# Decode attention with a gated unit on one core: keys multiplied in whole blocks, values by four columns of weights, the gate's weights late

## The chip, the cores and the metric

The kernel runs on one core of a Trainium2 chip. The metric is the device time of one execution in microseconds. Three runs of the kernel before took 719.57, 720.96 and 721.34 us; the median is 720.96.

## The reference

One token passes a block of attention over a cache and a gated unit; the product of the two is added to the input. All is in 32-bit floats.

```python
xn = layernorm(x)                                        # x: 1 x 512
q  = (xn @ wq).reshape(32, 128)                          # 32 heads of 128
p  = softmax(einsum("hd,hkd->hk", q, k_cache) * 128**-0.5)   # 8192 keys a head
s  = einsum("hk,hkd->hd", p, v_cache).reshape(4096) @ wo # 4096 x 512
h  = sigmoid(xn @ w_gate) * (xn @ w_up)                  # 512 x 1376 each
g  = silu(h @ w_down)                                    # 1376 x 512
out = x + s * g
```

K and V caches have 4096 KB for each head, 268.4 MB in all; the weights add 25.2 MB (wq and wo 8.39 MB each, the three of the gated unit 8.46 MB together).

## The kernel before

All large inputs pass through one pool of six slots (`stream`, 128 partitions x 32 KB): a slot holds one head's K, one head's V, half of `wq`, half of `wo`, or one of the three weights of the gated unit. SyncE issues every load, in the order in which the program names them, and stops at a load for which no slot is free; the loads behind it then stop too. The order is x, both halves of `wq`, `w_gate`, `w_up`, `w_down`, then K and V head by head, with K of the last two heads ahead of their V, and `wo` in two halves last. The second half of `wo` is cut into three loads. `need` issues along this order up to the item that is asked for; at head h the program asks for K of head h + 2.

A tile of K has 64 rows of keys in each partition (128 x 64 = 8192 keys), 128 elements each. The engines' instructions are issued in the order of the program (`manual_schedule`); semaphores between them come from the accesses to tiles.

For the start, VectorE and TensorE normalise x, TensorE multiplies it with `wq` (L152) and spreads four heads' queries at a time over all partitions (`spread`, L159 to L165). The gated unit follows as a whole: 11 blocks of columns of each of the two weights are loaded into TensorE as 128 x 128 blocks and multiplied by one column (L179), then sigmoid and product, and the product with `w_down` (L189 to L193).

Then the heads run, a head's second part behind the first quarter of the next head's scores:

- `scores` (L205 to L212): for each of the 64 rows of keys VectorE multiplies by the query and sums up in one fused operation (L211), which puts the products into a scratch tile and one score per partition into `sc`; the profile shows it as two instructions, the operation and a read of its sum.
- `row_max` and `all_max` (L214 to L228): the maximum of a partition's scores, TensorE's transpose of these 128 values, their maximum, its spread over the partitions, and ScalarE's exponential with the sum of each partition.
- `values` (L230 to L246): the total of the sums by a product with ones (`pl`), its reciprocal, and 64 products, each with one column of `pr` as weights (loaded into TensorE) and 128 columns of V moving; four groups of TensorE's columns take them in turn. ScalarE copies the four partial rows, and four small products with the reciprocal turn them into a column (`o_all`).

In the last step `project` multiplies the 32 heads with `wo` (L251, 128 products), and VectorE multiplies by the gate and adds x (L300, L301). The heads' order and the six slots set what TensorE, VectorE and the loads may do at one time: a slot of K comes free behind the last score of its head, a slot of V behind the last of its 64 products.

## Time and profile before

| | before |
|---|---|
| median of three runs | 720.96 us |
| profiled execution, its own time | 719.32 us |
| span of the profile, first to last instruction | 717.5 us |
| TensorE matmuls, busy | 334.6 us, 47% |
| VectorE, busy | 460.1 us, 64% |
| ScalarE, busy | 43.6 us, 6% |
| bytes read from the memory | 293.67 MB, 409 GB/s over the span |
| mean granted TensorE clock | 0.650 of full speed |

Times of the rows below count from the start of the span. A group's row gives line, engine, operation, the tiles out<-in, shapes and count, then busy time, mean duration of one in ns, and the idle time of the engine before it with what ended it. PE is TensorE's matmul, PEld its weight load, DVE VectorE, ACT ScalarE, SPq SyncE's queue. A matmul of 32-bit floats shows as two instructions.

### The profile page before, as it was taken

Reading aid. Unit: us, or ns where it says so; the run is one execution under the profiler, and the core shown is the slowest. Engines: PE = TensorE matmul, PEld = TensorE weight load, DVE = VectorE, ACT = ScalarE, POOL = GpSimd, SP = SyncE. Lnnn points to the kernel's source line nnn. Section 1 sums busy time; section 2 is a strip of 40 time slices with the busy share of each in tenths; the row PEclk is TensorE's granted clock in tenths of the full one; section 3 lists DMA queues with packets and bytes.
Section 4 is the critical chain, followed back from the end, with each engine's and each line's share of the span. In section 5 each row is a group of like instructions: output and inputs, shape, how many; then the busy total and the mean of one; then the engine's idle time right before and its main releaser. Section 6 shows DMA issues by size and latency. Waiting matters only on the chain.

```text
span 717.5 us, 15014 instructions
## 1 busy us (share of the span) xinstructions
PE 334.6 (47%) x5148; PEld 233.7 (33%) x5148; DVE 460.1 (64%) x4213; ACT 43.6 (6%) x177; POOL 0.7 (0%) x6
## 2 busy tenths in 40 slices
PE   3799155455444453235444453335444442234466
PEld 1499033333233332122333332223333221222345
DVE  1000888887767766667677666677677666676860
ACT  0100010000000000000000000000000000000000
POOL 0000000000000000000000000000000000000000
PEclk9855556655666666666665555555555666666659
DMA  9999999999999999999999999999999999999930
GB/s 378 419 433 434 428 425 432 436 435 425 431 429 435 432 429 427 436 429 438 426 427 434 432 434 427 431 432 434 429 431 427 436 432 432 407 424 420 400 158 21
DMA packets 11500, 294.63 MB, mean 411 GB/s; under 512 B 1336, under 2 KB 1344, under 8 KB 1696
## 3 DMA queue, kind: packets, MB, share of 16 engines
q1 hardware_dynamic: 11424, 293.68, 95.6%
q8 instruction: 40, 0.66, 0.3%
q14 instruction: 36, 0.29, 0.1%
HBM read 293.67 MB, written 0.00 MB: 409 GB/s over the span
## 4 chain that ended last, share of the span: by engine, by line
DMA 64%; DVE 24%; PE 9%; ACT 1%; issue 1%; SPq 0%; DVEq 0%
DMA k<-in_A_k_cache_dram 55%; DVE junk L211 22%; PE pgu L179 5%; DMA wo<-in_A_wo_dram 5%; DMA wg<-in_B_w_gate_dram 4%; PE pl L232 1%; PE pm L224 1%; DVE sc L211 1%; ACT pr L228 1%; PE po L237 1%; PE pd L189 1%; PE acc L251 1%; DVE mx L222 0%; ACT mx L225 0%; DVE rl L234 0%
## 5 line engine op out<-in xcount | busy, mean ns | idle before, releaser
L211 DVE CUSTOM_DVE_ANT_0 junk<-k,qb 128x128 f32<-128x128 f32 x2048 | 439.7, 288 | 99.8 <-DMA k<-in_A_k_cache_dram 99.8
L237 PE MATMUL po<-v,pr 128*1 128x128 f32 x4096 | 184.1, 362 | 0.0
L211 DVE DVE_READ_ACCUMULATOR2_ANT sc<- 128x1 f32 x2048 | 170.2, 83 | 0.1
L237 PEld LDWEIGHTS po<-v,pr 128*1 128x1 f32 x4096 | 126.4, 110 | 48.8 <-issue 0.2
L224 PE MATMUL pm<-mx,ones 1*128 1x1 f32 x64 | 18.6, 357 | 182.9 <-DVE mx L222 182.9
L224 PEld LDWEIGHTS pm<-mx,ones 1*128 1x128 f32 x64 | 15.9, 306 | 205.5 <-DVE mx L222 205.5
L218 PE MATMUL pt<-ident,mx 128*1 128x128 f32 x64 | 17.6, 375 | 138.7 <-DVE mx L216 138.7
L218 PEld LDWEIGHTS pt<-ident,mx 128*1 128x1 f32 x64 | 2.8, 80 | 141.8 <-DVE mx L216 126.2
L234 DVE RECIPROCAL rl<-pl 128x1 f32<-128x1 f32 x32 | 5.4, 169 | 65.0 <-PE pl L232 65.0
L183 DVE TENSOR_TENSOR hid<-hid,pgu 128x10 f32<-128x10 f32 (+1 forms) x2 | 0.3, 159 | 62.6 <-ACT hid L182 62.6
L232 PE MATMUL pl<-rs,ones 128*128 128x1 f32 x64 | 18.7, 362 | 24.7 <-ACT pr L228 24.7
L245 PE MATMUL pT<-rl,o 128*32 128x1 f32 x256 | 20.5, 201 | 12.6 <-ACT o L240 12.6
L245 PEld LDWEIGHTS pT<-rl,o 128*32 128x32 f32 x256 | 17.8, 154 | 22.0 <-ACT o L240 22.0
L232 PEld LDWEIGHTS pl<-rs,ones 128*128 128x128 f32 x64 | 16.0, 310 | 27.5 <-ACT pr L228 27.5
L225 ACT ACTIVATE mx<-pm 128x1 f32<-128x1 f32 x32 | 5.5, 171 | 318.8 <-PE pm L224 318.8
L240 ACT COPY o<-po 128x128 f32<-128x128 f32 x32 | 8.5, 266 | 204.7 <-PE po L237 204.7
L179 PEld LDWEIGHTS pgu<-xn,wg 128*128 128x128 f32 (+1 forms) x88 | 19.4, 316 | 1.1 <-ACT q_row L155 1.1
L179 PE MATMUL pgu<-xn,wg 128*128 128x1 f32 (+1 forms) x88 | 19.5, 358 | 0.3 <-DMA wg<-in_B_w_gate_dram 0.3
L179 PE MATMUL pgu<-xn,wu 128*128 128x1 f32 (+1 forms) x88 | 19.5, 358 | 0.0
L179 PEld LDWEIGHTS pgu<-xn,wu 128*128 128x128 f32 (+1 forms) x88 | 19.4, 317 | 0.0
L152 PE MATMUL pq<-wq,xn 128*1 128x512 f32 x64 | 10.3, 800 | 13.6 <-DMA wq<-in_A_wq_dram 13.6
L162 PE MATMUL pb<-q_row,ones 1*128 1x512 f32 x16 | 15.6, 1074 | 0.0
(46 smaller groups left out, 83.4 us busy)
## 6 DMA issues: line engine op xcount, KB each, us to landing
k<-in_A_k_cache_dram SPq DMA_DIRECT2D x32, 4096.0 KB, 44.7
v<-in_A_v_cache_dram SPq DMA_DIRECT2D x32, 4096.0 KB, 38.7
wq<-in_A_wq_dram SPq DMA_DIRECT2D x2, 4096.0 KB, 16.6
wo<-in_A_wo_dram SPq DMA_DIRECT2D x1, 4096.0 KB, 44.8
wo<-in_A_wo_dram SPq DMA_DIRECT2D x1, 3072.0 KB, 36.8
wg<-in_B_w_gate_dram SPq DMA_DIRECT2D x1, 2752.0 KB
wu<-in_B_w_up_dram SPq DMA_DIRECT2D x1, 2752.0 KB, 34.1
wd<-in_B_w_down_dram SPq DMA_DIRECT2D x1, 2560.0 KB, 40.0
```

What stands on the lines that cost most here:

```text
L152: nc.tensor.matmul(pq[b][g * GP:g * GP + 1, :], xn[:, k:k + 1], wq_t[k][:, c:c + QT], start=(k == 0), stop=(k == KT - 1))
L162: nc.tensor.matmul(pb, ones[g * GP:g * GP + 1, :], q_row[g * GP:g * GP + 1, b, :], start=True, stop=True)
L179: nc.tensor.matmul(pgu[:m, a * NT + t:a * NT + t + 1], gl[name, k][:, cols], xn[:, k:k + 1], start=(k == 0), stop=(k == KT - 1))
L189: nc.tensor.matmul(pd[g * GP:g * GP + 1, :GC], hid[:m, t:t + 1], gl["wd", t][:m, g * GC:(g + 1) * GC], start=(t == 0), stop=(t == NT - 1))
L211: nc.vector.tensor_tensor_reduce(junk, kv_t["k", h][:, j, :], q, 1.0, 0.0, ALU.mult, ALU.add, sc[h][:, j:j + 1])
L218: nc.tensor.matmul(pt, mx[h][:, 0:1], ident, start=True, stop=True)
L224: nc.tensor.matmul(pm, ones[:1, :], mx[h][:1, 1:2], start=True, stop=True)
L228: nc.scalar.activation(pr[h], sc[h], AF.Exp, bias=mx[h][:, 2:3], scale=SCALE, accum_out=rs[h])
L232: nc.tensor.matmul(pl, ones, rs[h], start=True, stop=True)
L237: nc.tensor.matmul(po[h % 2][g * GP:g * GP + 1, :], pr[h][:, j:j + 1], kv_t["v", h][:, j, :], start=(j < NG), stop=(j >= NB - NG))
L240: nc.scalar.copy(o1, po[h % 2])
L245: nc.tensor.matmul(pT[rows, r:r + 1], o1[:, r:Dh:R], rl[h], start=True, stop=True)
```

## The change

- The fused operation on 128 elements is replaced by two on 16 rows of keys at once: a product of 2048 elements written in place over the K tile, with the query repeated by a stride of zero, and a sum over each of the 16 rows. A head has four such pairs (SB = 16).
- The values take four columns of `pr` as weights and 512 columns of V moving, 16 products a head. Each gives four rows, of which only the diagonal blocks are wanted; four products with `pick`, which has a one at the wanted row of each group, add these up into one partition of `pn`, one for each of four heads. The sums go into a column of the same tile. Every fourth head `heads_out` divides, and VectorE's own transposes make the column `o_all`.
- The gated unit's weights are loaded between the heads, behind V of heads 20, 21 and 22; its products run between heads 21 and 25, with xn as weights and the columns of `w_gate` and `w_up` moving. Sigmoid and product use spare room in the slots of these two weights. K and V of the first two heads follow `wq` at once.
- The load of x as rows comes late, behind most of `wo`, and the last load of `wo` is cut at partition 120. `wo` stays last. The small tiles of PSUM have one buffer in place of three.

```diff
--- before.py
+++ after.py
@@ -35,17 +35,16 @@
...
+    SB = 16
-    R = 4
-    NW = H // R
-    FT = F // P
-    FL = F - FT * P
+    NW = H // HT
     SCALE = float(Dh) ** -0.5
+    GLU = 20
...
-    ps_s = ctx.enter_context(tc.tile_pool(name="ps_s", bufs=3, space=bass.MemoryType.PSUM))
+    ps_s = ctx.enter_context(tc.tile_pool(name="ps_s", bufs=1, space=bass.MemoryType.PSUM))

...
     def load_gate(name, src):
-        t = slot(name)[:, :KT * F].rearrange("p (k f) -> p k f", f=F)
+        t = slot(name)
+        gl[name, "spare"] = t[:, KT * F:KT * F + QT]
+        t = t[:, :KT * F].rearrange("p (k f) -> p k f", f=F)
         nc.sync.dma_start(t, src.rearrange("(p k) f -> p k f", k=KT))
         for k in range(KT):
             gl[name, k] = t[:, k, :]

+
...
     def load_down():
...
+        t = slot("wd")[:, :NF * D].rearrange("p (c e) -> p c e", e=D)
+        c = 0
+        for f0, m, r in FB:
+            nc.sync.dma_start(t[:m, c:c + r, :],
+                              w_down[f0:f0 + m * r, :].rearrange("(p r) e -> p r e", r=r))
+            c += r
+        gl["wd"] = t

     def load_rows(which, src, h):
         t = slot(f"{which}{h}")
         nc.sync.dma_start(t, src[0, h].rearrange("(p j) d -> p (j d)", p=P))
...
+        if last:
+            nc.sync.dma_start(t[:, m, :HT - 1, :], src[:, m, :HT - 1, :])
+            nc.sync.dma_start(x_row[0:P:GP, :], xv.rearrange("(g c) -> g c", g=NG))
+            for p0, p1 in ((0, 120), (120, P)):
+                nc.sync.dma_start(t[p0:p1, m, HT - 1, :], src[p0:p1, m, HT - 1, :])
...
+    order = [("wq", 0), ("wq", 1)]
+    for h in range(H):
+        order.append(("k", h))
+        if h < H - 2:
+            order.append(("v", h))
+        if GLU <= h < GLU + 3:
+            order.append(("glu", h - GLU))
+    order += [("v", H - 2), ("v", H - 1), ("wo", 0), ("wo", NW // 2)]
+
+    def issue(which, i):
+        if which == "wq":
+            load_wq(i)
+        elif which == "wo":
+            load_wo(i, NW // 2, i > 0)
+        elif which == "glu":
+            (lambda: load_gate("wg", w_gate), lambda: load_gate("wu", w_up), load_down)[i]()
+        else:
+            load_rows(which, k_cache if which == "k" else v_cache, i)
+
...
     nc.sync.dma_start(x_col, xv.rearrange("(p k) -> p k", k=KT))
-    load_wq(0)
-    nc.vector.memset(x_row, 0.0)
-    nc.sync.dma_start(x_row[0:P:GP, :], xv.rearrange("(g c) -> g c", g=NG))
-    load_wq(1)
-    load_gate("wg", w_gate)
-    load_gate("wu", w_up)
-    load_down()
+    need("v", 1)


...
+    nc.vector.memset(x_row, 0.0)

...
-    hid = const.tile([P, FT + 1], F32, name="hid")
+
     g_row = const.tile([P, GC], F32, name="g_row")
-    pgu = ps_big.tile([P, 512], F32, tag="ps_big", name="pgu")
-    NT = FT + 1
-    for a, name in enumerate(("wg", "wu")):
-        for t in range(NT):
-            m = P if t < FT else FL
-            cols = slice(t, FT * P, FT) if t < FT else slice(FT * P, F)
-            for k in range(KT):
-                nc.tensor.matmul(pgu[:m, a * NT + t:a * NT + t + 1], gl[name, k][:, cols], xn[:, k:k + 1],
+    pgu = {}
+
+    def glu_row(name):
+        pgu[name] = big(f"p{name}", 0.0)
+        for k in range(KT):
+            for n, f0 in enumerate(range(0, F, QT)):
+                w = min(QT, F - f0)
+                nc.tensor.matmul(pgu[name][n * GP:n * GP + 1, :w], xn[:, k:k + 1], gl[name, k][:, f0:f0 + w],
                                  start=(k == 0), stop=(k == KT - 1))
-    for rows, c0, c1 in ((P, 0, FT), (FL, FT, NT)):
-        nc.scalar.activation(hid[:rows, c0:c1], pgu[:rows, c0:c1], AF.Sigmoid)
-        nc.vector.tensor_mul(hid[:rows, c0:c1], hid[:rows, c0:c1], pgu[:rows, NT + c0:NT + c1])
-    pd = ps_big.tile([P, 512], F32, tag="ps_big", name="pd")
-    nc.vector.memset(pd[:, :GC], 0.0)
-    for t in range(NT):
-        m = P if t < FT else FL
-        for g in range(NG):
-            nc.tensor.matmul(pd[g * GP:g * GP + 1, :GC], hid[:m, t:t + 1],
-                             gl["wd", t][:m, g * GC:(g + 1) * GC],
-                             start=(t == 0), stop=(t == NT - 1))
-    nc.scalar.activation(g_row, pd[:, :GC], AF.Sigmoid)
-    nc.vector.tensor_mul(g_row, g_row, pd[:, :GC])
+
+    def glu_hidden():
+        nc.scalar.activation(gl["wg", "spare"], pgu["wg"], AF.Sigmoid)
+        nc.vector.tensor_mul(gl["wu", "spare"], gl["wg", "spare"], pgu["wu"])
+
+    def glu_out():
+        ph = big("ph")
+        hid = const.tile([P, NF], F32, name="hid")
+        c = 0
+        for f0, m, r in FB:
+            n, o = divmod(f0, QT)
+            row = gl["wu", "spare"][n * GP:n * GP + 1]
+            for t in range(r):
+                nc.tensor.matmul(ph[:m, c + t:c + t + 1], row[:, o + t:o + m * r:r],
+                                 ones[n * GP:n * GP + 1, 0:1], start=True, stop=True)
+            nc.scalar.copy(hid[:m, c:c + r], ph[:m, c:c + r])
+            c += r
+        pd = big("pd", 0.0)
+        c = 0
+        for f0, m, r in FB:
+            for t in range(c, c + r):
+                for g in range(NG):
+                    nc.tensor.matmul(pd[g * GP:g * GP + 1, :GC], hid[:m, t:t + 1],
+                                     gl["wd"][:m, t, g * GC:(g + 1) * GC],
+                                     start=(t == 0), stop=(t == NF - 1))
+            c += r
+        nc.scalar.activation(g_row, pd[:, :GC], AF.Sigmoid)
+        return pd


     acc = ps_acc.tile([P, GC], F32, name="acc")
     nc.vector.memset(acc, 0.0)
-    po = [ps_o.tile([P, Dh], F32, name=f"po{i}") for i in range(2)]
+    po = [ps_o.tile([P, QT], F32, name=f"po{i}") for i in range(2)]
+
+    pn = [ps_o.tile([P, Dh + 1], F32, name=f"pn{i}") for i in range(2)]
     for t in po:
         nc.vector.memset(t, 0.0)
-
-    o_all = const.tile([P, NW, R], F32, name="o_all")
-    sc, mx, pr, rs, rl = {}, {}, {}, {}, {}
+    for t in pn:
+        nc.vector.memset(t, 0.0)
+        nc.vector.memset(t[:, Dh:], 1.0)
+
+    o_all = const.tile([P, NW, HT], F32, name="o_all")
+
+    pick = const.tile([P, HT], F32, name="pick")
+    nc.vector.memset(pick, 0.0)
+    for g in range(NG):
+        nc.vector.tensor_copy(pick[g * GP:(g + 1) * GP, :], ident[g * GP:(g + 1) * GP, g * GP:g * GP + HT])
+    sc, mx, pr, rs = {}, {}, {}, {}

     def scores(h, j0, j1):
         if j0 == 0:
             sc[h] = work.tile([P, NB], F32, tag="sc", name=f"sc{h}")
-        q = qb[h // HT][:, (h % HT) * Dh:(h % HT + 1) * Dh]
-        for j in range(j0, j1):
-            junk = work.tile([P, Dh], F32, tag="junk", name=f"junk{h}_{j}")
-            nc.vector.tensor_tensor_reduce(junk, kv_t["k", h][:, j, :], q, 1.0, 0.0, ALU.mult, ALU.add,
-                                           sc[h][:, j:j + 1])
+        q = qb[h // HT][:, (h % HT) * Dh:(h % HT + 1) * Dh].rearrange("p (o d) -> p o d", o=1)
+        q = q.to_broadcast([P, SB, Dh])
+        for j in range(j0, j1, SB):
+            kt = kv_t["k", h].rearrange("p (j d) -> p j d", d=Dh)[:, j:j + SB, :]
+            nc.vector.tensor_mul(kt, kt, q)
+            nc.vector.reduce_sum(sc[h][:, j:j + SB], kt, axis=AX.X)

     def row_max(h):
         mx[h] = work.tile([P, 4], F32, tag="mx", name=f"mx{h}")
@@ -228,71 +292,70 @@
         nc.scalar.activation(pr[h], sc[h], AF.Exp, bias=mx[h][:, 2:3], scale=SCALE, accum_out=rs[h])

     def values(h):
-        pl = ps_s.tile([P, 1], F32, tag="ps_s", name=f"pl{h}")
-        nc.tensor.matmul(pl, ones, rs[h], start=True, stop=True)
-        rl[h] = work.tile([P, 1], F32, tag="rl", name=f"rl{h}")
-        nc.vector.reciprocal(rl[h], pl)
-        for j in range(NB):
-            g = j % NG
-            nc.tensor.matmul(po[h % 2][g * GP:g * GP + 1, :], pr[h][:, j:j + 1], kv_t["v", h][:, j, :],
-                             start=(j < NG), stop=(j >= NB - NG))
-        o1 = work.tile([P, Dh], F32, tag="o1", name=f"o1_{h}")
+        w, i = divmod(h, HT)
+        row = pn[w % 2][i * GP:i * GP + 1, :]
+        nc.tensor.matmul(row[:, Dh:], rs[h], ones[:, 0:1], start=True, stop=True)
+
+        for j in range(0, NB, HT):
+            g = j // HT % NG
+            nc.tensor.matmul(po[h % 2][g * GP:g * GP + HT, :], pr[h][:, j:j + HT],
+                             kv_t["v", h][:, j * Dh:(j + HT) * Dh],
+                             start=(j < HT * NG), stop=(j >= NB - HT * NG))
+        o1 = work.tile([P, QT], F32, tag="o1", name=f"o1_{h}", bufs=1)
         nc.scalar.copy(o1, po[h % 2])
-        w, i = divmod(h, R)
-        pT = ps_s.tile([P, R], F32, tag="ps_s", name=f"pT{h}")
-        rows = slice(i * GP, (i + 1) * GP)
-        for r in range(R):
-            nc.tensor.matmul(pT[rows, r:r + 1], o1[:, r:Dh:R], rl[h], start=True, stop=True)
-        nc.scalar.copy(o_all[rows, w, :], pT[rows, :])
+        for b in range(HT):
+            nc.tensor.matmul(row[:, :Dh], pick[:, b:b + 1], o1[:, b * Dh:(b + 1) * Dh],
+                             start=(b == 0), stop=(b == HT - 1))
+
+    def heads_out(w):
+        rl = work.tile([P, 1], F32, tag="rl", name=f"rl{w}")
+        nc.vector.reciprocal(rl, pn[w % 2][:, Dh:])
+        on = work.tile([P, Dh], F32, tag="on", name=f"on{w}", bufs=1)
+        nc.vector.tensor_scalar(on, pn[w % 2][:, :Dh], rl, None, op0=ALU.mult)
+        ot = work.tile([P, HT, GP], F32, tag="ot", name=f"ot{w}", bufs=1)
+        for r in range(HT):
+            nc.vector.transpose(ot[:, r, :], on[:, r:Dh:HT])
+        nc.vector.tensor_copy(o_all[:, w, :], ot[:, :, 0])

     def project(w):
-        for r in range(R):
+        for r in range(HT):
             for g in range(NG):
                 nc.tensor.matmul(acc[g * GP:g * GP + 1, :], o_all[:, w, r:r + 1],
                                  wo_t[w][:, r, g * GC:(g + 1) * GC],
-                                 start=(w + r == 0), stop=(w == NW - 1 and r == R - 1))
-
-
-    order = []
+                                 start=(w + r == 0), stop=(w == NW - 1 and r == HT - 1))
+
+
+    spread(0)
+    pt = pd = None
     for h in range(H):
-        order.append(("k", h))
-        if h < H - 2:
-            order.append(("v", h))
-    order += [("v", H - 2), ("v", H - 1), ("wo", 0), ("wo", NW // 2)]
-
-    def issue(item):
-        which, i = item
-        if which == "wo":
-            load_wo(i, NW // 2, () if i == 0 else ((0, R - 1), (R - 1, R)))
-        else:
-            load_rows(which, k_cache if which == "k" else v_cache, i)
-
-    ahead = iter(order)
-    loaded = set()
-
-    def need(item):
-        while item not in loaded:
-            nxt = next(ahead)
-            issue(nxt)
-            loaded.add(nxt)
-
-    pt = None
-    for h in range(H):
-        need(("k", h))
+        need("k", h)
         if h + 2 < H:
-            need(("k", h + 2))
+            need("k", h + 2)
         if h % HT == HT - 2 and h + HT < H:
             spread(h // HT + 1)
-        scores(h, 0, NB // 4)
+        scores(h, 0, SB)
         if h > 0:
             all_max(h - 1, pt)
-            need(("v", h - 1))
+            if h % HT == 1 and h > 1:
+                heads_out(h // HT - 1)
+            need("v", h - 1)
             values(h - 1)
-        scores(h, NB // 4, NB)
+        scores(h, SB, NB)
         pt = row_max(h)
-    need(order[-1])
+        if h == GLU + 1:
+            glu_row("wg")
+        elif h == GLU + 2:
+            glu_row("wu")
+        elif h == GLU + 3:
+            glu_hidden()
+        elif h == GLU + 4:
+            pd = glu_out()
+        elif h == GLU + 5:
+            nc.vector.tensor_mul(g_row, g_row, pd[:, :GC])
+    need(*order[-1])
     all_max(H - 1, pt)
     values(H - 1)
+    heads_out(NW - 1)
     for w in range(NW):
         project(w)

```

## Rows read from the trace of the kernel before

**Rows 1.** Busy time of each engine, clock and transfers in two stretches.

```profile
core 0: us, PE busy (x) PEld busy (x) DVE busy (x) ACT busy (x) POOL busy (x), PEclk, DMA share, GB/s
500.00:600.00 100.00, 42.97 (x712) 28.72 (x712) 71.27 (x655) 5.74 (x26) 0.00 (x0) 0.62 1.00 431
692.00:710.00 18.00, 11.71 (x270) 8.91 (x270) 3.53 (x31) 1.03 (x5) 0.00 (x0) 0.72 0.07 30
```

**Rows 2.** Timeline of SyncE's queue: start us, us, what; two issues of K.

```profile
556.87 0.33 SPq L91 DMA_DIRECT2D k<-in_A_k_cache_dram  x1
...
577.18 0.33 SPq L91 DMA_DIRECT2D k<-in_A_k_cache_dram  x1
```

**Rows 3.** Chain that ended last, from head 30 on: start us, us, what.

```profile
617.78 44.73 DMA k<-in_A_k_cache_dram
...
662.64 0.29 DVE junk L211
...
673.66 36.81 DMA wo<-in_A_wo_dram
...
710.51 3.72 PE acc L251 x128
```

**Rows 4.** Loads by tile: KB each, median us from issue to landing.

```profile
x_col<-in_A_x_dram SPq DMA_DIRECT2D x1, 2.0 KB, 1.6
```

**Rows 5.** The page: engines' busy us (share) xinstructions; transfer queues: packets, MB, share.

```profile
PE 334.6 (47%) x5148; PEld 233.7 (33%) x5148; DVE 460.1 (64%) x4213; ACT 43.6 (6%) x177; POOL 0.7 (0%) x6
...
q8 instruction: 40, 0.66, 0.3%
q14 instruction: 36, 0.29, 0.1%
```

**Rows 6.** Groups by line and operation on VectorE and ScalarE.

```profile
L211 DVE CUSTOM_DVE_ANT_0 junk<-k,qb 128x128 f32<-128x128 f32 x2048 | 439.7, 288 | 99.8 <-DMA k<-in_A_k_cache_dram 99.8
...
L211 DVE DVE_READ_ACCUMULATOR2_ANT sc<- 128x1 f32 x2048 | 170.2, 83 | 0.1
...
L222 DVE TENSOR_REDUCE mx<-pt 1x1 f32<-1x128 f32 x32 | 8.8, 274 | 0.7 <-PE pt L218 0.7
...
L216 DVE TENSOR_REDUCE mx<-sc 128x1 f32<-128x64 f32 x32 | 7.0, 220 | 1.1
...
L165 ACT COPY qb<-pb 128x512 f32<-128x512 f32 x8 | 4.7, 586 | 44.3 <-PE pb L162 44.3
...
L301 DVE TENSOR_TENSOR res<-res,x_row 128x128 f32<-128x128 f32 x1 | 0.3, 291 | 0.0
...
L133 DVE TENSOR_TENSOR sq<-xc 128x4 f32<-128x4 f32 x1 | 0.2, 164 | 0.0
...
L134 DVE TENSOR_REDUCE st<-sq 128x1 f32<-128x4 f32 x1 | 0.2, 157 | 0.0
```

**Rows 7.** Timeline of VectorE: the first score, and two neighbours in head 31.

```profile
75.65 0.27 DVE L211 CUSTOM_DVE_ANT_0 junk<-k,qb 128x128 f32<-128x128 f32 x1
...
681.38 0.29 DVE L211 CUSTOM_DVE_ANT_0 junk<-k,qb 128x128 f32<-128x128 f32 x1
...
681.59 0.29 DVE L211 CUSTOM_DVE_ANT_0 junk<-k,qb 128x128 f32<-128x128 f32 x1
```

**Rows 8.** Timeline of the end, behind the last score.

```profile
694.89 0.22 DVE L216 TENSOR_REDUCE mx<-sc 128x1 f32<-128x64 f32 x1
...
697.95 5.87 PE L237 MATMUL po<-v,pr 128*1 128x128 f32 x128
...
704.69 3.68 PE L251 MATMUL acc<-wo,o_all 128*1 128x128 f32 x122
...
714.26 0.29 DVE L300 TENSOR_TENSOR res<-g_row,acc 128x128 f32<-128x128 f32 x1 [16.03 <-PE acc L251]
714.58 0.29 DVE L301 TENSOR_TENSOR res<-res,x_row 128x128 f32<-128x128 f32 x1
```

**Rows 9.** Timeline of TensorE: the second half of the query product.

```profile
23.22 5.29 PE L152 MATMUL pq<-wq,xn 128*1 128x512 f32 x32 [4.62 <-DMA wq<-in_A_wq_dram]
```

More of the change, by code (lines that the diff above doesn't have):

```diff
@@ L80, in load_gate @@
             gl[name, k] = t[:, k, :]
-    def load_down():
-        t = slot("wd")[:, :(FT + 1) * D].rearrange("p (t e) -> p t e", e=D)
-        nc.sync.dma_start(t[:, :FT, :], w_down[:FT * P, :].rearrange("(p t) e -> p t e", t=FT))
-        nc.sync.dma_start(t[:FL, FT, :], w_down[FT * P:F, :])
-        for i in range(FT + 1):
-            gl["wd", i] = t[:, i, :]
+    FB, f0 = [], 0
+    while f0 < F:
+        n = min(QT, F - f0) if f0 % QT == 0 else (f0 // QT + 1) * QT - f0
+        n = min(n, F - f0)
+        m = P if n >= P and n % P == 0 else 96 if n >= 96 else n
+        FB.append((f0, m, n // m))
+        f0 += m * (n // m)
+    NF = sum(r for _, _, r in FB)
+    def load_down():
+        t = slot("wd")[:, :NF * D].rearrange("p (c e) -> p c e", e=D)
[5 more added lines that the diff above has]
+        gl["wd"] = t
     def load_rows(which, src, h):
@@ L91, in load_rows @@
         nc.sync.dma_start(t, src[0, h].rearrange("(p j) d -> p (j d)", p=P))
[L92 to L100 removed]
+        kv_t[which, h] = t
@@ new lines, in load_wo @@
+    def load_wo(g0, n, last):
+        t = slot(f"wo{g0}").rearrange("p (g r e) -> p g r e", r=HT, e=D)
+        src = wo[g0 * P * HT:(g0 + n) * P * HT, :].rearrange("(g p r) e -> p g r e", p=P, r=HT)
+        m = n - 1 if last else n
+        nc.sync.dma_start(t[:, :m], src[:, :m])
+        if last:
[3 more added lines that the diff above has]
+                nc.sync.dma_start(t[p0:p1, m, HT - 1, :], src[p0:p1, m, HT - 1, :])
@@ new lines, with need @@
+    order += [("v", H - 2), ("v", H - 1), ("wo", 0), ("wo", NW // 2)]
[8 more added lines that the diff above has]
+            load_rows(which, k_cache if which == "k" else v_cache, i)
+    ahead = iter(order)
+    loaded = set()
+    def need(*item):
+        while item not in loaded:
+            nxt = next(ahead)
+            issue(*nxt)
+            loaded.add(nxt)
@@ L139, with big @@
     nc.vector.tensor_scalar(xn, xc, st[:, 4:5], None, op0=ALU.mult)
-    q_row = const.tile([P, NQ // NG, QT], F32, name="q_row")
-    pq = []
-    for b in range(NQ // NG):
-        t = ps_big.tile([P, QT], F32, tag="ps_big", name=f"pq{b}")
-        nc.vector.memset(t, 0.0)
-        pq.append(t)
+    def big(name, fill=None):
+        t = ps_big.tile([P, QT], F32, tag="ps_big", name=name)
+        if fill is not None:
+            nc.vector.memset(t, fill)
+        return t
+    q_row = const.tile([P, NQ // NG, QT], F32, name="q_row")
+    pq = [big(f"pq{b}", 0.0) for b in range(NQ // NG)]
     for k in range(KT):
@@ L160, in spread @@
         b, g = divmod(t, NG)
-        pb = ps_big.tile([P, QT], F32, tag="ps_big", name=f"pb{t}")
+        pb = big(f"pb{t}")
         nc.tensor.matmul(pb, ones[g * GP:g * GP + 1, :], q_row[g * GP:g * GP + 1, b, :],
```

8 lines of the change are left out of this document (removed).

## Prediction

> **What bounds the kernel now.** I read the share of busy time first, then the transfer rate by stage, the queue of SyncE, the chain that ended last, and the tail of the timeline. No compute engine is near full, and the transfer engines are: between 500 and 600 us they move 431 GB/s [rows 1]. One head brings a K and a V transfer, 2 x 4096 KB = 8.389 MB, which at that rate takes 19.46 us. But SyncE issues K transfers 20.30 us apart (556.87, 577.18, 617.78, that is 60.91 us for three heads) [rows 2, 3]. A head costs 0.84 us more than its bytes. The reader finds the missing time at the end: from 692 to 710 us the rate is 30 GB/s, about one sixteenth of 431 (26.9) [rows 1]. One of the 16 transfer engines is still busy 18 us after the others, and a transfer counts as landed only when its slowest part has.
>
> The same by bytes: up to the K tile of head 30, 272.7 MB are due (query weights 8.39, gate weights 8.46, 31 K and 30 V tiles). At 431 GB/s that is 632.7 us; the first bytes can move at about 2.5 us (a tiny load takes 1.6 us to land [rows 4]), so K of head 30 could land at 635.2. It was waited for until 662.5 [rows 3]: 27.3 us late.
>
> What does the late engine carry besides? The queues show loads that the program never issues, of kind "instruction": 40 packets of 16 KB on queue 8 and 36 of 8 KB on queue 14 [rows 5]. 0.66 MB over TensorE's 10,296 instructions is 64 B each; 0.29 MB over VectorE's 4,213 is 69 B [rows 5]. So these are the programs of the two engines, and a head, with its 64 fused operations and 64 reads of their sum on VectorE [rows 6], needs about one packet of queue 14 and 1.25 of queue 8. Per packet they took 0.32 us (0.1% of 16 x 717.5 us over 36) and 0.86 us. A loss of 0.84 us a head lies between 0.32 and 1.25 x 0.86 = 1.07. No row names the engine; that instruction loads make it late is my inference.
>
> **The change, part by part.** *Fewer instructions.* Per head VectorE's 128 instructions become 8, with maxima and the per-four-heads normalisation some 12; TensorE's 256 for the values become 64, with the small ones some 92. If the lateness goes with VectorE's loads it falls to about a tenth, 3 us; if with TensorE's, to 0.4 of it, 11 us; if with neither it stays at 27 (rival C). I take 5: the packets of queue 14 come one a head, as the loss does. K of head 30, with the same bytes ahead of it, then lands at 635.2 + 5 = 640.2.
>
> *VectorE pays for it.* The fused operation takes a new 128 elements every 0.21 us [rows 7]: 64 x 0.21 = 13.6 us a head. Now each element passes twice, four times a head through a multiply and a sum of 2,048 elements. A multiply of 4 elements took 164 ns, one of 128 took 291: 1.02 ns an element, so 291 + 1,920 x 1.02 = 2.26 us for 2,048. A sum of 4 took 157 ns, a maximum of 64 took 220: 1.05 ns an element, 2.30 us for 2,048 [rows 6]. A dependent operation starts 0.03 us after the one before it [rows 8]. I take 4.55 us a pair, 18.2 a head. Bounds of a pair: 4.3, when nothing is fixed (2 x 2,048 x 1.05), and 6.8, when every 128 elements of either pass cost the 0.21 us of today; it is the long stream of elements that makes the small rows grow, so I stay near the lower end. With the two maxima (0.22 and 0.27 [rows 6]) and gaps a head is 18.75 us, and 0.4 more for the normalisation, which comes every fourth head (seven short operations of 0.16 to 0.29): 19.1. The stream would need 19.46 + 0.16 = 19.6. VectorE goes from two thirds busy to almost full, yet still follows the transfers by half a us a head. The normalisation makes VectorE wait for TensorE's picks of the head before last, with three quarters of a head's scores queued behind; they end in the head between, some 4 us ahead of need, so it costs nothing until VectorE or the values are that much later.
>
> *Values by four columns.* 64 x 128 moving columns become 16 x 512, the same 8,192. Thirty-two matmul instructions of that shape took 5.29 us in the query product [rows 9], against 5.87 for the last head's 128 today [rows 8]. The copy, four times as wide, is 0.59 us [rows 6], the picks about 1.0 (8 instructions). Under VectorE's 18.75 this hides, save in the last head.
>
> *The gate's weights late.* The product with them, the 42 us that kept the first scores until 75.65 [rows 7], leaves the start: scores begin at about 33 us, when the queries and the first K (12.6 MB at 431 GB/s) are there. It is needed: 75.65 + 32 x 19.1 = 687 would be the end of the scores by VectorE alone. Behind head 20 the three loads come between K and V and keep three of the six slots until heads 23 and 24 are scored. K of head 24 then waits for the slot of V of head 22, free about 4.55 + 0.3 + 1.5 + 5.3 = 11.7 us after K of head 23 lands (first pair, maximum, exponential chain, values); plus up to 1.6 us to the first bytes [rows 4] is 13.3. The stream is through with V of head 23 9.7 us after K's last byte, and K's landing is seen a little after that byte. I price the stall at 5 us (0 to 10, as the slots fall). The gate's products, its sigmoid and two more table loads lie on TensorE and ScalarE, under the scores; VectorE's four clears and products (some 3 us) fall where K arrives 6.5 us a head later anyhow, because the gate's bytes are in between. So K of head 30 lands at 645.2.
>
> *The tail.* K of head 31 comes right behind it, so two heads of scores follow: 645.2 + 2 x 18.75 = 682.7. Then today's steps: from the maximum to the first value 3.06 us (694.89 to 697.95), values 5.29, copy 0.6, picks 1.0, the projection 3.68 + 3.72 and from its end to the end of the span 3.3 [rows 3, 8]: 20.6. The span ends at 703.3. By transfers alone: five more behind K of head 30, 20.97 MB in 48.7 us, so 693.9, and 7.0 from landing to the end (710.5 to 717.5) [rows 3]: 700.9. The scores decide, by 2.4 us; loading x late and cutting the last output weights finer lie on the other arm and cost nothing.
>
> Sum: span 703.3, against 717.5 now. The profiled execution's own time is 1.8 us over its span (719.32) and the runs' median 1.6 above that: **706.5 us** predicted against 720.96.
>
> **The rivals.** *A, the forecast*: 698 to 715. Ends: lateness 3 or 11 (-2, +6), stall 0 or 10 (-5, +5, and without it the transfer arm holds at about 699), a pair of 4.4 or 4.7 (-1, +2).
>
> *B, slower: VectorE becomes the bound.* Place: the multiply and sum of every head. If a head costs VectorE more than the stream's 19.6 us, K waits in its slots and each head pays. The end is then 33 + 32P + 20.6 + 3.4, and it passes 721 at P = 20.75, a pair of 4.95 us, 9% over my 4.55. With the sum alone at 0.21 us per 128 elements a pair is 2.3 + 3.4 = 5.7, P = 23.75 and the time 817; with both 6.8, P = 28.15, 958. For it: no row shows a sum with 16 results, a broadcast operand or an in-place product. Against it: every row grows by one ns an element, whatever it reads.
>
> *C, slower: instruction loads are not what makes one engine late.* Then K of head 30 still lands at 662.5, the fuller VectorE makes the tail longer, and the time is 662.5 + 37.5 + 20.6 + 3.4 = 724, up to 729 with the stall. For it: no row ties the loads to the late engine, and an engine slow in itself would look alike. Against it: the 27.3 us is the size of one of the two queues on one engine (34 or 11 us of packets). The Trainium skill, "Runtime: NRT & Kernel Launch", section "Instruction fetch mechanics", states that fetching the next block of instructions is mostly hidden; by that rule this rival holds. The trace shows only that the loads exist and run on the transfer queues.
>
> *D, the slots cost more.* If the three gate tiles let the stream run dry for 20 us rather than 5, the time is 721: no gain. Against it: K arrives in steps of 26 us there, and VectorE, at 19, has time to free slots.
>
> **How the numbers follow.** Chances: A 0.77, B 0.10, C 0.07, D 0.06. About 0.3% (2 us) is what a measurement can tell from no change. Faster takes A and half of B's lower end and of D: 0.81. The same, 718.8 to 723.1, takes a part of D, B and C: 0.06. Slower: 0.13. The likeliest one's time is given; the range goes to 697 below, where the stall is gone and the lateness 3, and to 719 above, where a pair of 4.9 or a stall of 17 would stand; it leaves out less than two in ten.
>
> **What would show it.** Right: K issues 19.5 to 19.7 us apart outside heads 20 to 25; VectorE 85% busy or more, pairs near 4.55; some 4 to 6 packets of 8 KB; no stretch in which one transfer engine works alone for more than some 5 us; the end a chain of two heads' scores, values and projection. The stall: K of head 24 over 3 us behind its bytes. Wrong: a pair over 4.95 with VectorE never idle (B), K issues still 20.3 apart with few instruction packets (C), or SyncE waiting for gate slots for tens of us (D).

## The result and the profile after

The changed kernel takes 708.86 us (median of four runs, 708.47 to 709.38), the kernel before 720.40 beside it: a ratio of 0.984, 95% interval 0.9823 to 0.9857. The forecast was 706.5 in 697 to 719. The profiled run is the one of 709.38 us.

First the page of the changed kernel: busy time of each engine, the queues of instruction loads, the costliest groups.

```profile
PE 311.6 (44%) x1980; PEld 95.0 (13%) x1980; DVE 606.7 (86%) x407; ACT 53.7 (8%) x151; POOL 0.7 (0%) x6
...
q8 instruction: 15, 0.25, 0.1%
q14 instruction: 6, 0.05, 0.0%
...
L275 DVE TENSOR_TENSOR k<-k,qb 128x2048 f32<-128x2048 f32 x128 | 292.1, 2282 | 69.1 <-DMA k<-in_A_k_cache_dram 69.1
L276 DVE TENSOR_REDUCE sc<-k 128x16 f32<-128x2048 f32 x128 | 292.6, 2286 | 6.4
L301 PE MATMUL po<-v,pr 128*4 128x512 f32 x1024 | 185.6, 888 | 0.0
```

VectorE went from 4,213 instructions to 407 and from 64% busy to 86%; queue 14 from 36 packets to 6, queue 8 from 40 to 15 [rows 5]. The reader should look next at what the stream gained. SyncE's issues of K of heads 8 and 20:

```profile
151.15 0.33 SPq L104 DMA_DIRECT2D k<-in_A_k_cache_dram  x1
...
384.84 0.33 SPq L104 DMA_DIRECT2D k<-in_A_k_cache_dram  x1
```

That is 233.69 us for 12 heads, 19.47 a head, against 20.30 [rows 2, 3]: the bytes' own 19.46. But the chain that ended last is not even behind head 20, where the gate's weights come in:

```profile
384.84 38.57 DMA k<-in_A_k_cache_dram
...
487.78 18.18 DMA k<-in_A_k_cache_dram
...
512.80 5.79 PE po L301 x30
...
518.61 12.12 DMA k<-in_A_k_cache_dram
...
589.61 39.86 DMA k<-in_A_k_cache_dram
...
686.39 0.23 DVE mx L280
...
689.10 6.38 PE po L301 x30
...
697.18 7.00 PE acc L323 x247
```

K of head 20 landed at 423.41, K of head 29 at 629.47. Between them 83.96 MB are due (9 K, 9 V, 8.46 MB of the gate), 194.8 us at 431 GB/s; it took 206.1. The windows there (engines' busy us, clock, DMA share, GB/s) show two holes:

```profile
486.00:488.00 2.00, 1.71 (x16) 0.20 (x8) 1.97 (x2) 0.22 (x1) 0.00 (x0) 0.86 1.01 418
488.00:490.00 2.00, 1.03 (x8) 0.59 (x8) 2.00 (x2) 0.37 (x1) 0.00 (x0) 1.00 1.09 238
490.00:492.00 2.00, 0.00 (x0) 0.00 (x0) 1.97 (x2) 0.00 (x0) 0.00 (x0) 1.00 1.26 258
492.00:494.00 2.00, 0.00 (x0) 0.00 (x0) 1.97 (x2) 0.00 (x0) 0.00 (x0) 0.85 1.26 321
494.00:496.00 2.00, 1.82 (x9) 0.54 (x12) 0.61 (x2) 0.00 (x0) 0.00 (x0) 0.50 0.73 286
...
512.00:516.00 4.00, 3.37 (x18) 0.64 (x22) 3.96 (x3) 0.55 (x3) 0.00 (x0) 0.50 0.23 98
516.00:518.00 2.00, 2.00 (x20) 0.44 (x12) 1.98 (x1) 0.00 (x0) 0.00 (x0) 0.68 0.00 0
```

From 488 to 496 the rate is 238 to 321 GB/s, 2.9 us behind 431. There the last of w_down's four loads move (rows of 6 and 2 KB a partition, on 96 and 64 partitions) and the first bytes of K of head 23; from 484 to 488 the rows of 8 KB of w_down still moved at 393 and 418 GB/s. From 512 to 518 the stream is nearly dry: K of head 24 could be issued only at 518.61, when TensorE was done with V of head 22. At the end the scores decide, as forecast: VectorE is busy from K of head 29 to 686.39, and the projection (697.18) waits for no load. Three heads of scores follow each other there without a wait, behind K of head 29. No transfer engine works alone for long: the rate is 347 GB/s from 694 to 696 us, 93 from 696 to 698 and 0 from 698 to 700.

### The profile page after: what moved, and what is told of

Same layout as the page of the kernel before. It is cut to its first block, busy times and chain, and to the rows that moved or that the text cites. A ratio compares the mean times of both kernels' runs of the same rounds, so it can differ in the third digit from the quotient of the medians.

```text
span 707.5 us, 4802 instructions
## 1 busy us (share of the span) xinstructions
PE 311.6 (44%) x1980; PEld 95.0 (13%) x1980; DVE 606.7 (86%) x407; ACT 53.7 (8%) x151; POOL 0.7 (0%) x6
## 4 chain that ended last, share of the span: by engine, by line
DMA 53%; DVE 41%; PE 4%; issue 1%; ACT 0%; SPq 0%; another core or an unknown queue 0%; DVEq 0%
DMA k<-in_A_k_cache_dram 53%; DVE sc L276 20%; DVE k L275 20%; PE po L301 3%; PE acc L323 1%; DVE mx L286 0%; DVE ot L317 0%; DVE on L314 0%; PE pm L288 0%; DVE mx L280 0%; ACT pr L292 0%; PE pn L307 0%; SPq L104 0%; DVE o_all L318 0%
## 5 line engine op out<-in xcount | busy, mean ns | idle before, releaser
L275 DVE TENSOR_TENSOR k<-k,qb 128x2048 f32<-128x2048 f32 x128 | 292.1, 2282 | 69.1 <-DMA k<-in_A_k_cache_dram 69.1
L276 DVE TENSOR_REDUCE sc<-k 128x16 f32<-128x2048 f32 x128 | 292.6, 2286 | 6.4
L301 PE MATMUL po<-v,pr 128*4 128x512 f32 x1024 | 185.6, 888 | 0.0
L301 PEld LDWEIGHTS po<-v,pr 128*4 128x4 f32 x1024 | 34.0, 111 | 119.7 <-issue 119.7
L307 PE MATMUL pn<-o,pick 128*1 128x128 f32 x256 | 33.1, 272 | 22.8 <-ACT o L305 22.8
L305 ACT COPY o<-po 128x512 f32<-128x512 f32 x32 | 18.8, 586 | 189.8 <-PE po L301 189.8
L307 PEld LDWEIGHTS pn<-o,pick 128*1 128x1 f32 x256 | 18.8, 83 | 59.5 <-ACT o L305 54.7
L292 ACT ACTIVATE pr<-sc,mx 128x64 f32<-128x64 f32 x32 | 11.2, 349 | 1.0
L286 DVE TENSOR_REDUCE mx<-pt 1x1 f32<-1x128 f32 x32 | 8.6, 268 | 0.7 <-PE pt L282 0.7
L323 PE MATMUL acc<-wo,o_all 128*1 128x128 f32 x256 | 7.6, 272 | 0.0
```

What stands on the lines that cost most here:

```text
L275: nc.vector.tensor_mul(kt, kt, q)
L276: nc.vector.reduce_sum(sc[h][:, j:j + SB], kt, axis=AX.X)
L292: nc.scalar.activation(pr[h], sc[h], AF.Exp, bias=mx[h][:, 2:3], scale=SCALE, accum_out=rs[h])
L301: nc.tensor.matmul(po[h % 2][g * GP:g * GP + HT, :], pr[h][:, j:j + HT], kv_t["v", h][:, j * Dh:(j + HT) * Dh], start=(j < HT * NG), stop= ...
L305: nc.scalar.copy(o1, po[h % 2])
L307: nc.tensor.matmul(row[:, :Dh], pick[:, b:b + 1], o1[:, b * Dh:(b + 1) * Dh], start=(b == 0), stop=(b == HT - 1))
```

## The experiments

**One theory and its rivals.** Theory 1: the late transfer engine was late through the loads of VectorE's instructions. Theory 2: through TensorE's. Theory 3: the loads don't matter.

**Fused scores, one junk tile** (`junk = work.tile(..., bufs=1)`, for lack of memory).

```diff
-            nc.vector.tensor_mul(kt, kt, q)
-            nc.vector.reduce_sum(sc[h][:, j:j + SB], kt, axis=AX.X)
+            nc.vector.tensor_tensor_reduce(junk, k_j, q, 1.0, 0.0, ALU.mult, ALU.add, sc[h][:, j:j + 1])
```

> The changed kernel, but with the scores as before: 64 fused multiply-and-sum operations of 128 elements a head (and the 64 reads of their sums) in place of four pairs. Values, gate, order of loads and tail stay as changed. Theory 1 (VectorE's instruction loads make one transfer engine late): about 36 packets of kind instruction come back on queue 14, K issues stand 20.3 us apart again outside the gate's stretch instead of 19.4 to 19.5, K of head 30 lands at 662 or later, and although a head's scores cost VectorE only some 14.4 us the time is 720 to 731 us. Theory 2 (TensorE's loads, which stay at 15 packets) and theory 3 (loads don't matter, the pair or the clock of something else does): K issues stay 19.4 to 19.5 us apart, K of head 30 lands before 650, the two last heads take 9 us less than now, and the time is 700 to 705 us, faster than the changed kernel.

Measured: 761.8 us (ratio 1.0585, 1.055 to 1.062), outside both expectations. VectorE's timeline says why:

```profile
562.15 0.29 DVE L274 CUSTOM_DVE_ANT_0 junk<-k,qb 128x128 f32<-128x128 f32 x1
562.36 0.08 DVE L274 DVE_READ_ACCUMULATOR2_ANT sc<- 128x1 f32 x1
562.48 0.29 DVE L274 CUSTOM_DVE_ANT_0 junk<-k,qb 128x128 f32<-128x128 f32 x1
```

With one junk tile each operation waits for the one before it: 0.33 us apart, not 0.21 [rows 7], 21.5 us a head. VectorE was the bound, and the run doesn't test the theories. It was run again with room for two tiles.

**Fused scores, two junk tiles** (the last product written into `g_row`).

> The run with fused scores again, now with two junk tiles in turn as in the kernel before (the last product is written into the gate's row, which makes room for the second). Each fused operation should then start 0.21 us after the one before it and not 0.33, a head costs VectorE some 14.4 us, and the stream decides. Theory 1 (VectorE's instruction loads make one transfer engine late): about 35 packets on queue 14, K issues 20.2 to 20.4 us apart where VectorE isn't the bound, K of head 30 at about 635 + 25 + 8 = 668, the end by the transfers' arm at 668 + 49 + 7 = 724 and a time of 720 to 729 us. Rival (the lateness belongs to something else of the kernel before, and only went with it): K issues 19.4 to 19.6 us apart and a time of 700 to 706 us.

**Values by one column.**

```diff
-        for j in range(0, NB, HT):
-            nc.tensor.matmul(po[...][g * GP:g * GP + HT, :], pr[h][:, j:j + HT], v[:, j * Dh:(j + HT) * Dh], ...)
+        for j in range(NB):
+            nc.tensor.matmul(po[...][g * GP:g * GP + 1, :Dh], pr[h][:, j:j + 1], v[:, j * Dh:(j + 1) * Dh], ...)
```

> The changed kernel, but with the values by one column of weights times 128 columns: 64 matmuls of 128 columns a head, a copy of 128 columns, and one matmul with a column of ones in place of the four picks. Scores, gate, loads as changed. TensorE's instructions go back to some two thirds of what they were before. Theory 1 (VectorE's loads): queue 14 stays at 6 packets, queue 8 grows to 25 or more, K issues stay 19.4 to 19.5 us apart, the time is 707 to 710 us, the same as changed. Theory 2 (TensorE's loads): K issues 20.0 to 20.3 us apart and a time of 720 to 734 us. Theory 3: as theory 1.

**Sixty-four small copies more per head on ScalarE.**

```diff
+        for _ in range(n):
+            nc.scalar.copy(speck[:, 1:2], speck[:, 0:1])
```

> The changed kernel with 64 copies of one element more per head on ScalarE (24 behind the exponential, 40 behind the copy of the values), which nothing waits for but ScalarE's own next step; the results don't use them. Each should take about 0.2 us, 13 us of a head's 19.5, in gaps that ScalarE has. Theory 1 in its general form (the instruction loads of any engine that fall on one transfer engine cost the stream): a new instruction queue with some 16 packets of 8 KB, K issues 19.8 to 19.9 us apart (half of the 0.84 us, as 64 is half of the 128 instructions taken from VectorE), a time of 717 to 722 us. Theory 1 in its narrow form (VectorE's queue alone, for its place or its size): K issues stay 19.4 to 19.5 us apart, 708 to 711 us. Theory 3 (loads don't matter): 708 to 711 us too, and then also no return of the 20.3 us in the run with fused scores.

**Fused scores in every second head** (`if h % 2 == 0`, two junk tiles).

> The changed kernel with the fused operation (two junk tiles in turn) in every second head, pairs in the others: half the dose of the run with two junk tiles. Theory 1: some 20 packets on queue 14, K issues on the mean half-way between 19.47 us (6 packets) and 20.45 (35 packets), that is 19.9 to 20.0, and a time half-way between 709 and 731, 717 to 723 us. Rival (a packet costs what it cost in the run with ScalarE's copies, 0.30 us a head for 16 packets): 19.7 to 19.8 us and 712 to 716. Rival (the lateness comes with the fused operation as such only when it fills every head): below 19.6 us and 707 to 711.

Pages of the four, in this order: the lines of the two instruction queues (packets, MB, share).

```profile
q8 instruction: 15, 0.25, 0.1%
q14 instruction: 35, 0.29, 0.1%
```
```profile
q8 instruction: 37, 0.61, 0.3%
q14 instruction: 6, 0.05, 0.0%
```
```profile
q8 instruction: 15, 0.25, 0.1%
q14 instruction: 22, 0.18, 0.1%
```
```profile
q8 instruction: 15, 0.25, 0.1%
q14 instruction: 21, 0.17, 0.1%
```

And SyncE's issues of K of heads 8 and 20 in the run with two junk tiles:

```profile
150.15 0.33 SPq L104 DMA_DIRECT2D k<-in_A_k_cache_dram  x1
...
396.11 0.33 SPq L104 DMA_DIRECT2D k<-in_A_k_cache_dram  x1
```

The same two issues in every run, divided by 12:

| run | packets, queue 14 / 8 | K of head 8, 20 issued, us | us a head | median us | ratio to before (95%) |
|---|---|---|---|---|---|
| changed | 6 / 15 | 151.15, 384.84 | 19.47 | 708.86 | 0.984 (0.9823 to 0.9857) |
| every second head fused | 21 / 15 | 152.39, 392.52 | 20.01 | 718.79 | 0.9989 (0.9972 to 1.0006) |
| all heads fused | 35 / 15 | 150.15, 396.11 | 20.50 | 731.36 | 1.0151 (1.0128 to 1.0174) |
| ScalarE's copies | 22 / 15 | 151.18, 388.58 | 19.78 | 713.66 | 0.9918 (0.9903 to 0.9933) |
| values by one column | 6 / 37 | 151.25, 387.44 | 19.68 | 710.74 | 0.9881 (0.9866 to 0.9896) |

What follows. The interval between two heads' K issues grows with the packets: 15 of VectorE's give 0.54 us a head, 29 give 1.03, in proportion. In those runs VectorE is less busy than in the changed kernel (75% and 64%), so it isn't the bound. With every second head fused interval and time (20.01, 718.79 us) are those of half the dose, as theory 1 expected. With all heads fused K of head 30 landed at 672.98 and the time came out 2 us over what theory 1 expected; at the end of that run the rate is 26 GB/s from 718 to 722 us (the last number of the row), one engine alone again, as in [rows 1]:

```profile
718.00:722.00 4.00, 1.47 (x48) 1.08 (x40) 0.00 (x0) 0.00 (x0) 0.00 (x0) 0.93 0.06 26
```

ScalarE's copies, which touch neither a K tile nor VectorE, bring 16 packets of queue 14 and 0.31 us a head with them: theory 3 falls, and queue 14 carries ScalarE's programs too. The interval is just under the 19.8 to 19.9 us that the general form of theory 1 expected; the time, 713.66 us, lies between the two forms' ranges. It doesn't measure the loads alone: behind the last score ScalarE is still at the copies, and the last exponential starts some 1.9 us late. TensorE's 22 packets of 16 KB cost 0.21 us a head and the time 1.9 us, just over the 707 to 710 us of theory 1: theory 2 isn't nothing, but it is the small part. Per packet that is 1.1 us for VectorE's (1.03 over 29 packets in 31 heads), 0.6 for ScalarE's, 0.3 for TensorE's. Each interval is from one profiled execution, so the small prices are rough.

The records of single transfers in the traces say where most of this goes. With all heads fused a packet of VectorE's instructions takes 0.33 us, and the 32 KB packet that starts as it ends takes 1.88 us, where the others take 1.22: it costs its engine 0.99 us. A head's K and V are 16 packets of 32 KB for each engine, 19.5 us; with one such packet a head that makes the 20.50. A packet of ScalarE's copies takes 0.31 us and the next one 1.59, together 0.68. In the kernel before VectorE's take 0.31 us and the next one 1.84, beside 1.21 for the others: 19.4 and 0.94 us make about its 20.30. TensorE's packets are longer (1.06 us, and 1.71 for the next, with the values by one column), but as far as start and end times tell the engines apart they fall on different engines, and VectorE's mostly on one, which at 400 us is some 14 packets of 32 KB behind the rest. So what counts is what falls on one engine. Why the next packet is slower stays open.

**The gate first**: its loads behind the query weights, its new products ahead of the scores.

```diff
-    order = [("wq", 0), ("wq", 1)]
+    order = [("wq", 0), ("wq", 1), ("glu", 0), ("glu", 1), ("glu", 2)]
...
+    glu_row("wg"); glu_row("wu"); glu_hidden(); pd = glu_out()
```

> The changed kernel with the gate's three loads at the start (behind the query weights, ahead of K of head 0) and its products ahead of the first scores, as new instructions; everything else as changed. The first scores begin some 18 us later, near 52 us, and no slot is held later. Theory 1 (the gate's stretch costs the stream 11.3 us where it stands now, 6 of them because K of head 24 waits for a slot and the rest because w_down's four loads of short rows move slowly): the 6 us go and the slow rows only move, so K of head 30 lands near 642, the last score ends near 680, the span is 700 to 702 and the time 702 to 704 us; if the slow rows too belong to the place, 697 to 699. Rival (the prediction's own sentence that the late gate is needed because VectorE's 32 heads would otherwise decide): the last score stays at 686 or later and the time at 708 or above.

Measured: 701.23 us (0.9744, 0.9729 to 0.9758). The chain:

```profile
581.63 39.43 DMA k<-in_A_k_cache_dram
```

K of head 29 lands at 621.06 against 629.47, behind the same bytes, although the first score starts at 55.06 instead of 32.9. The late place cost 8.4 us there and 7.6 us of the time, and the rival falls. Theory 1 had priced the place at 6 us and expected 702 to 704 us; the gain is larger.

**w_down in long rows**, at the late place and, next, with the gate first.

```diff
-        for f0, m, r in FB:
-            nc.sync.dma_start(t[:m, c:c + r, :], w_down[f0:f0 + m * r, :].rearrange("(p r) e -> p r e", r=r))
+        nc.sync.dma_start(t[:, :FT, :], w_down[:FT * P, :].rearrange("(p t) e -> p t e", t=FT))
+        nc.sync.dma_start(t[:FL, FT, :], w_down[FT * P:F, :])
```

> The changed kernel with w_down loaded as before, 1,280 rows as ten a partition (20 KB at a time) and 96 rows of 2 KB, in place of four loads of 8, 8, 6 and 2 KB a partition; the products with w_gate and w_up take their columns in the order that fits, so nothing else changes. Theory 1: the slow stretch (some 8 us at 238 to 321 GB/s, 2.9 us lost) is the short rows' own; it goes, K of head 24 and all behind it come 2 to 3 us earlier, and the time is 705.5 to 707 us. Rival (the dry stream at K of head 24 is set by the slots alone and takes the gain back, or the rate there is low for another reason): 708 to 710 us.

> The gate first, as in the run of that name, and w_down in long rows. Theory 1: with the gate first the transfers decide each head until the last two, so the 1.5 to 3 us of the short rows come off the end as well: first scores at 52 to 53.5 us instead of 55.06, time 698 to 700 us. Rival (the end is held by VectorE's own work, so an earlier K only makes it wait): 700.7 to 701.7 us as with the gate first alone.

Measured: 706.77 us (0.9813, 0.9796 to 0.983) at the late place, 699.43 (0.9711, 0.9696 to 0.9725) with the gate first: 2.1 and 1.8 us less than without the edit, both in the ranges of theory 1. The first pair of intervals still overlaps, the second doesn't. At the late place the slow stretch, which here too has rows of 2 KB in it, is milder, 330 to 376 GB/s from 488 to 494 us, and a part of the gain goes into a longer dry hole (0 GB/s from 512 to 516).

**The scores alone**, in the kernel before: early gate with its old products, values by one column.

```diff
-            nc.vector.tensor_tensor_reduce(junk, kv_t["k", h][:, j, :], q, 1.0, 0.0, ...)
+            nc.vector.tensor_mul(kt, kt, q)
+            nc.vector.reduce_sum(sc[h][:, j:j + NB // 4], kt, axis=AX.X)
```

> The kernel before with one part of the change alone: the scores by four multiplies and sums of 2,048 elements a head. The gate's weights and products stay at the start, the values stay at one column of weights. The prediction's own sentence (the late gate is needed, since scores that begin at 75.65 us would end at 687 by VectorE alone) gives 687 + 23 for the tail of before + 1.8 = 711 to 712 us. Theory now: a head costs VectorE 18.6 to 18.8 us and not 19.1, so by VectorE alone the scores end near 676; queue 14 falls to some 6 packets, queue 8 keeps about 40, which cost the stream 0.2 us a head by the run with one column; K of head 30 lands at 640 to 645, the scores end at 677 to 683 and the time is 701 to 708 us, not slower than the whole change, because the gate's stretch (8 us) isn't paid. If VectorE's loads aren't the cause, 720 us or more.

Measured: 759.97 us (1.0549, 1.0532 to 1.0565). The ranges of 711 to 712 and 701 to 708 us missed, by some 50 us. The number lies in the third, 720 or more, but not for its reason: queue 14 had 6 packets here. The page's group for the reciprocal, the same group on the page of the kernel before, and the place on VectorE's timeline (in brackets idle time and who ended it):

```profile
L235 DVE RECIPROCAL rl<-pl 128x1 f32<-128x1 f32 x32 | 5.4, 168 | 64.9 <-PE pl L233 64.9
```
```profile
L234 DVE RECIPROCAL rl<-pl 128x1 f32<-128x1 f32 x32 | 5.4, 169 | 65.0 <-PE pl L232 65.0
```
```profile
307.01 0.27 DVE L223 TENSOR_REDUCE mx<-pt 1x1 f32<-1x128 f32 x1
309.26 0.17 DVE L235 RECIPROCAL rl<-pl 128x1 f32<-128x1 f32 x1 [1.99 <-PE pl L233]
309.35 2.27 DVE L212 TENSOR_TENSOR k<-k,qb 128x2048 f32<-128x2048 f32 x1
```

Once a head VectorE waits 1.99 us for TensorE's sum, with three pairs queued behind. A head costs 20.73 us, more than the stream's: VectorE becomes the bound, as in rival B, but through a wait and not through a slow pair. In the kernel before the same wait stood beside 99.8 us of waiting for K tiles [rows 6].

**The scores alone, the wait moved**: the values, and with them the reciprocal, behind the second pair.

```diff
         scores(h, 0, NB // 4)
         if h > 0:
             all_max(h - 1, pt)
+        scores(h, NB // 4, NB // 2)
+        if h > 0:
             need(("v", h - 1))
             values(h - 1)
-        scores(h, NB // 4, NB)
+        scores(h, NB // 2, NB)
```

> The run with the scores alone again, with the values of the head before (and with them the reciprocal of its sum on VectorE) emitted behind the second pair of a head and not behind the first. In the run before, VectorE stood 1.99 us a head in front of that reciprocal until TensorE's sum was there, with three pairs queued behind it: 20.73 us a head, 32 of them from 75.5 us. Theory: this wait, and not the early gate, made that run slow. With it gone a head costs 18.75 us, the scores end at 676 to 683 (the stream, with 40 packets on queue 8, decides at the upper end), and the time is 701 to 708 us, so that the late gate wasn't needed and is a loss. Rival (the early gate itself costs, by the 42 us in which VectorE has nothing to do): the prediction's 711 or more.

Measured: 700.10 us (0.9724, 0.971 to 0.974).

```profile
308.94 0.16 DVE L235 RECIPROCAL rl<-pl 128x1 f32<-128x1 f32 x1
309.01 2.27 DVE L212 TENSOR_TENSOR k<-k,qb 128x2048 f32<-128x2048 f32 x1
```

No idle time in front of the reciprocal. K issues stand 18.65 us apart until VectorE, which began at 76.24, has caught up with the stream near 540; then the K tiles decide. The time is a little below the 701 to 708 us expected. One edit and one moved line do better than the whole change, by 8.8 us.

**The tail.** Heads 30 and 31 by the fused operation, on top of gate first and long rows; then the last 3 MB load of output weights cut into three.

```diff
+        if h >= H - 2:
+            for j in range(j0, j1):
+                nc.vector.tensor_tensor_reduce(junk, k_j, q, 1.0, 0.0, ALU.mult, ALU.add, sc[h][:, j:j + 1])
+            return
...
+            for i in range(m):
+                nc.sync.dma_start(t[:, i], src[:, i])
```

> As the run before it, but heads 30 and 31 with the fused operation of the kernel before (0.21 us per 128 elements, two junk tiles in turn). Theory 1 (the end is decided by two heads of scores behind the K tiles, as the prediction has it): these two heads take some 2 x 4.2 us less, the end moves forward until the last output weights decide (their last byte and some 8 us of products), 1.5 to 5 us below the run before it: 694 to 698 us. Against it work two more packets of instructions late in the stream. Rival (the transfers' arm decides already): no gain, 698 to 701 us.

> As the run with the fused operation in the last two heads, but the load of 3 MB of the last output weights is cut into three of 1 MB, each for one step of the projection. In that run the first half of the projection is done at about 685.3 us, and the second half (5.25 us) waits for that load until 688.31. Theory (the transfers' arm decides there): two of the three steps run while the rest still lands, the end comes 2 to 3 us earlier, 695 to 696.5 us. Rival (the last bytes of all three land together, since one late engine holds a part of each): no gain, 697.5 to 699 us.

Measured: 698.20 us (0.9694, 0.9676 to 0.9713), which its interval doesn't tell from the 699.43 without: in the rival's range, and just above theory 1's. The scores end earlier, but the chain then runs over the last output weights, landed at 688.31 (651.26 + 37.01). With that load cut 696.49 (0.9673, 0.9658 to 0.9687), as its theory expected and the best median here; its interval still overlaps the one before. Its chain:

```profile
651.83 38.26 DMA wo<-in_A_wo_dram
...
690.23 1.24 PE acc L322 x32
```

The end now is the last output weights and 32 matmuls behind them: the transfers' arm decides, not the scores.

## Why the prediction was right

The mechanism was right in its main step, and the total within 2.4 us, in part by luck (see the sum). By its steps:

- *Fewer instructions.* Right, and shown by the dose above. "I take 5" for the lateness at head 30: with the gate first K of head 29 lands at 621.06, and by bytes it is due at 264.3 MB / 431 + 2.5 = 615.7, so 5.4 (4.1 with w_down in long rows, 619.82). The tie to VectorE's queue was too narrow: the queue is ScalarE's as well, and TensorE's takes a part. A packet's own 0.32 us, the lower bound of the price, was a third of it; the rest is the slower packet behind. The Trainium skill, "Runtime: NRT & Kernel Launch", section "Instruction fetch mechanics", has the fetch of a block mostly hidden. For the engine that runs the instructions no row here speaks against it; for a stream that fills the transfer engines these runs do, with up to 1.03 us a head. Rival C falls.
- *VectorE pays.* A pair takes 2.21 + 0.02 + 2.29 = 4.52 us (4.55), a head 18.6 (18.75). Rival B didn't come in the changed kernel, but its margin is thin: 2 us a head more, in the run with the scores alone, cost 40 us of time against before. What kept it off was the edit that I priced least, the normalisation moved one head on: I wrote that it costs nothing, and not that it takes away a wait of 1.99 us a head, which the kernel before already had (65.0 us over 32 heads on its page), where VectorE waited for K tiles anyhow. The two runs with the scores alone show that wait; in the changed kernel itself the edit was not taken back.
- *Values.* One column in place of four costs 1.9 us here, so the reshaping is worth that, most likely by TensorE's fewer instructions (19.47 us a head against 19.68); that cause was not isolated. In the last head they took 6.45 us, not 5.29: the granted clock was 0.55 there, most of it the lower level (1.2 GHz), behind 7 us (680 to 687) in which TensorE was busy for 1.4; in the query product that I took the figure from [rows 9] it was 0.68.
- *The gate's weights late: the step that failed.* "It is needed: 75.65 + 32 x 19.1 = 687" charges each head the 0.4 us of normalisation that is due every fourth head. With 18.65 us a head, scores that began at 76.24 ended at 678.6 in the run with the moved wait, 8 us ahead of the changed kernel's 686.6; with the gate first and all else as changed they ended at 678.3. The stall was forecast at 5 us (0 to 10). It is 8.4 for the place, within that range but above the 5, and the short rows of w_down, which I had at no cost, some 2 more, wherever they stand (2.1 late, 1.8 first). The place of the stall (K of head 24 behind V of head 22's slot) was right.
- *The tail.* From the last score to the end of the span 21.1 us, forecast 20.6; the scores' arm decides, right.
- *The sum.* Its last terms (703.3, 1.8 and 1.6) add up to 706.7, not 706.5. Last score 686.4 against 682.7 (the gate): three heads back to back behind K of head 29, not two behind K of head 30. Span 707.5 against 703.3. The profiled time lies 1.9 over the span (1.8); the median 0.5 under the profiled time, where I had added 1.6. This hid 2.1 of the 4.2 us, which was luck.

So the 11.5 us gained can be put together from some 19 for the scores, as the run without the rest of the change and with the moved wait has it (719.5 to 700.1), and some 2 for the values, less 9.4 that the late gate and the short rows of w_down give back (708.86 to 699.43). That the parts simply add was not tested, and the late load of x, the cut at partition 120 and the single PSUM buffers were not run alone. The best run, at 0.9673 of before, keeps the change's values and, in all but the last two heads, its scores; it undoes the gate's place, loads w_down in long rows and cuts the last output weights finer.

## What to carry to other kernels

Where the stream is the bound, count instructions on every engine: their loads ride on the same transfer engines, and one of 16 that is late sets the landing. Before an engine is filled to the stream's pace, list every wait in its queue: a wait of 2 us a head that the kernel before could hide, with VectorE 64% busy, cost 60 us here (759.97 against 700.10) once VectorE set the pace. And moving loads away from the start, so that an engine can begin earlier, is no gain if that engine catches up anyhow: compare its whole work with the time that is left.

## What was not expected of the hardware

- The fused operation ran 0.21 us apart with two result tiles in turn and 0.33 with one: a wait on the engine's own last operation costs 0.12 us each time.
- A packet of VectorE's instructions, 0.33 us on a transfer engine, made the 32 KB packet behind it 0.66 us longer (1.88 against 1.22).
- Sixty-four copies of one element a head on ScalarE came with 0.31 us a head more for the transfers; the kernel took 4.8 us longer, some 1.9 of them because the last exponential waited for copies.
- Where the loads of w_down end in rows of 6 and 2 KB a partition, the rate fell to 238 to 321 GB/s for 8 us; rows of 8 KB had moved at 393 to 418, K and V tiles move at 431. With rows of 20 KB, and 2 KB for the last 96, the slowest 6 us were at 330 to 376.
